# Plain output products set between the second block's first products of h, transposes ahead of the last rounding, and a pinned order with a pause on GpSimd

## The chip, the core and the metric

The kernel runs on one core of a Trainium2 chip. The core has TensorE (matrix products, PE in the profile; its weight loads are PEld), VectorE (DVE), ScalarE (ACT), GpSimd (POOL) and SyncE (SP), which here only issues DMAs. The metric is the device time of one execution in microseconds; lower is better.

## The reference

The input `x` is (8, 4096, 192), all float32. A causal convolution of 7 taps runs along the sequence, channel by channel, with one softmaxed set of taps for each of 8 heads; then a block of two matrices with silu between them:

```python
w = np.exp(weight - weight.max(-1, keepdims=True)); w = w / (w.sum(-1, keepdims=True) + 1e-9)
out = np.einsum('hk,bskhg->bshg', w, x_unf)      # 7 taps, zeros ahead of each sequence
h = out.reshape(32768, 192) @ w_in               # 192 -> 2048
g = h * (1.0 / (1.0 + np.exp(-h)))
return g @ w_out                                 # 2048 -> 192
```

The kernel takes the bits of the weights as they come, 64 bits to a word pair, and rounds them to float32 on the chip (`rounded`).

## The kernel before, in words

**Blocks.** The 32768 rows are 32 blocks of 1024 rows, each as two halves of 512 columns. For each block the rows are loaded (`ld`), transposed by VectorE so that channels lie on partitions (`i`, three of them), given the last 6 columns of the block before (`ha`, the halo: a copy and a small DMA), and convolved: tap 0 is ScalarE's, taps 1 to 6 are VectorE's (`v.ki` is tap i of channel part k; 18 on VectorE). The result is spread over both halves of the partitions by DMA (`sp.k`) and added up into five window sums (`w.0` to `w.5`).

**Products of h.** The first matrix is not multiplied plainly. Its 2048 columns are five groups (g = 0 to 4) and one plain piece; in each group 15 products (`Pr.g`) of combined weights with window sums or rows replace 18. A product has 64 rows of weights, so it occupies one half of TensorE's rows; the set `ON_B` (r = 0, 1, 2, 4, 5, 6, 11, 14, without 14 of group 4) says which products use the second half. The plain piece is `L`. The groups follow one another in the order of `QUEUE` (0, 4, 1, 2, 3). The products of a group build up in chains in PSUM, and between them ScalarE copies (`u`), VectorE adds (`X`, `a`, `b`, at L653) and ScalarE takes the silu (`S`, `SL`), which gives the tiles `g`. A bank of a group is written again two groups later, so a late addition holds up later products.

**Products of the output.** The second matrix is also combined: VectorE forms four differences for each quarter j of the columns (`t.ji`, L692), TensorE does six slots for each j and half e (`Di.je`, L724), and VectorE and ScalarE merge seven banks (`M`, `z`, `y`, `x`), transpose (`o`) and store (`st`).

**Block 0** goes another way, for the combined weights aren't ready: its convolution of the first two parts is done on TensorE (L977), its h by plain products (`up_plain`, L565, 192 records of TensorE), its output by plain products (`down_plain`, L743, 192 records). Meanwhile VectorE rounds the weights (`rounded`: four quarters of the input weights, then `round_out(0)` to `round_out(3)` for those of the output weights) and GpSimd combines them: 19 operations of 64x128 for each of five groups and 3 more for group 4 (`combine`), and 16 of 128x192 for the output weights (`combine_out`, which overwrite a part of `wo` that `down_plain` reads). All of GpSimd's combinations are at L353 (`comb`).

**The order** is written by hand. Each engine works through its own queue in the order in which the instructions were issued; instructions in `pin` keep the order of the program. `PLAN` is the steady order of one block's period; `START` is the order of the first blocks up to where `PLAN` begins. A token stands for block b = 2 in `START`; `-` ahead of it is block 1, `=` block 0 and `+` block 3, and the tokens that prepare input (`i`, `ha`, `v`, `sp`, `w`) act on the block after that. So `=v.21` is a tap of block 1, and `-P5.0` a product of block 1. `step` carries a token out. Before the change, `first_down` does all of block 0's plain output products at one place, when `START` comes to its first product; GpSimd's combinations are issued by `nc.gpsimd` without a pin, so that their place in GpSimd's queue is left to the scheduler.

Of the kernel before, what the change touches and what calls it, by code (L numbers as in the profile page):

```python
# [9 lines left out]
F32 = mybir.dt.float32  # L10
# [7 lines left out]
def kernel(  # L18
# [24 lines left out]
    nc = tc.nc  # L43
# [61 lines left out]
        "P7.3 | P11.3 b1.3 S3.3 sp.0 +v.10 | P8.2 a5.3"  # L105
    )
    START = (
        "=i.2 =i.0 =i.1 =ha.0 -ld.2 =v.00 =v.10 =v.01 -ld.1 =v.20 =v.11 =v.21 =v.12 -ld.0 "
        "=v.22 =v.23 =v.13 =v.14 =v.15 =v.02 =v.16 =v.24 =sp.1 =v.03 =v.25 =v.26 =v.04 =sp.2 "
        "=v.05 =v.06 -i.2 =sp.0 -i.0 ld.1 =w.0 =w.1 =o.0 -i.1 -L.01 -P5.0 =w.2 -ha.0 -L.02 "  # L110
        "-P5.4 -u5.0 =w.3 -P3.0 -P2.0 -u5.4 =w.5 =o.1 -L.00 -P2.4 -u4.0 =w.4 =st.1 -P6.0 "
        "-u4.4 -SL.0 -P6.4 -u2.0 -X2.0 -L.11 -u2.4 -L.10 -v.10 -P12.0 -P1.0 -v.11 -L.12 -u0.0 "
        "=o.2 -P9.0 -P1.4 -v.20 =st.2 -SL.2 -P13.0 -P0.0 -u0.4 -X4.0 -v.12 -P0.4 -P3.4 -u1.0 "
        "ld.0 -S2.0 -b1.0 -P7.0 -P14.0 -u1.4 -X2.4 -P11.0 -P10.0 -S3.0 -a5.0 =st.0 -P5.1 "
        "-P9.4 -S4.0 -b5.0 -v.13 -P12.4 -P4.0 -u5.1 ld.2 -X4.4 -v.00 -P2.1 -P14.4 -b1.4 -a1.0 "
        "-P7.4 -P11.4 -u4.1 -v.14 -S3.4 -P6.1 -P10.4 -S1.0 -v.21 -P8.0 -P5.2 -v.01 -u2.1 "
        "-S4.4 -a5.4 -P1.1 -P13.4 -u5.2 -a0.0 -SL.1 -P4.4 -b5.4 -u0.1 -P3.1 -S2.4 -P0.1 -a1.4 "
        "-P12.1 -X2.1 -P2.2 -u1.1 -v.22 -P9.1 -P14.1 -P8.4 -X4.1 -S3.1 -b1.1 -u4.2 -P7.1 "
        "-P5.3 -v.02 -S0.0 -P10.1 -P6.2 -a5.1 -a0.4 -P13.1 -P4.1 -u2.2 -v.23 -P3.2 -u5.3 "
        "-P1.2 -a1.1 -S2.1 -S0.4 -X2.2 -P2.3 -P8.1 -u0.2 -b5.1 -P11.1 -P9.2 -u4.3 -a0.1 -S1.1 "  # L120
        "-v.03 -P6.3 -P13.2 -S4.1 -P3.3 -P0.2 -X4.2 -u2.3 -v.04 -S2.2 -P12.2 -u1.2 -X2.3 "
        "-S5.0 -P7.2 -P11.2 -v.24 -S0.1 -P9.3 -P14.2 -b1.2 -S5.4 -a5.2 -S1.4 -P10.2 -P1.3 "
        "-S3.2 -v.25 -S5.1 -D0.00 -v.15 -S4.2 -v.05 -u0.3 -D1.00 -b5.2 -P0.3 -P13.3 -X4.3 "
        "-v.16 -P12.3 -P4.2 -u1.3 -t.00 -P11.3 -P7.3 -a1.2 -D1.20 -b1.3 -S1.2 -D0.11 -a5.3 "
        "-S2.3 -S4.3 -t.02 -D0.01 -S5.2 -D1.01 -v.26 -t.01 -D0.31 -v.06 -P10.3 -P14.3 -t.03 "
        "-P8.2 -P4.3 -S3.3 -sp.2 -D1.21 -a0.2 -a1.3 -D1.30 -b5.3 -sp.1 -D0.21 -t.10 -S5.3 "
        "-S0.2 -D4.00 i.1 -D3.01 i.0 +ld.2 i.2 -D4.01 -t.11 -D2.00 ha.0 -D2.01 -D0.20 -sp.0 "
        "-t.12 -D3.00 -t.13 v.00 -D5.00 v.20 P5.0 -P8.3 -D5.01 -a0.3 -D2.10 -t.20 -S0.3 +ld.0 "
        "-D5.11 -D4.10 -S1.3 v.21 v.10 -D1.10 u5.0 -w.0 -D2.11 -t.21 -D0.10 -w.1 -D3.10 v.01 "
        "v.11 -D4.11 -D5.10 -t.23 -D3.11 -D1.11 -t.22 -D4.21 v.12 -D2.21 -t.30 -D4.20 v.22 "  # L130
        "-D5.20 -D0.30 -t.31 -D2.20 -y0.0 v.02 P3.0 P2.0 -t.33 -D2.31 v.03 -D2.30 v.04 -D5.30 "
        "-w.2 -D1.31 -t.32 -D3.20 -w.3 -D5.31 -D5.21 v.23 -D4.30 -x2.0 u4.0 v.24 -D3.30 -x2.1 "
        "-z1.0 -w.4 -D3.31 -y2.0 -M1.0 -y1.0 -D3.21 v.05 -x2.2 -x0.0 -M3.0 P6.0 L.01 -M2.0 "
        "-D4.31 u2.0 -x2.3 X2.0 P12.0 P1.0 -M6.0 -w.5 P5.4 L.00 u0.0 -M4.0 L.02 P0.0 u5.4 "
        "v.25 P2.4 u1.0 b1.0 P14.0 u4.4 -M5.0 -x1.0 P6.4 P9.0 S3.0 v.13 P13.0 P5.1 u2.4 X4.0 "
        "SL.0 -o.1 P10.0 P1.4 S2.0 v.14 u5.1 L.11 b5.0 u0.4 L.12 v.06 L.10 P7.0 P0.4 v.15 "
        "SL.2 P12.4 P2.1 u1.4 a5.0 -M7.0 P11.0 P3.4 u4.1 P6.1 P14.4 S4.0 X2.4 S5.0 b1.4 P4.0 "
        "P13.4 u2.1 -o.2 S3.4 P1.1 P9.4 a1.0 v.16 P5.2 P8.0 u0.1 X4.4 P10.4 P0.1 u5.2 a0.0 "
        "P7.4 P2.2 b5.4 u1.1 S2.4 P3.1 P14.1 a5.4 u4.2 P12.1 P4.4 X2.1 S3.1 v.26 P11.4 P9.1 "
        "a1.4 P6.2 P13.1 -o.3 S4.4 X4.1 P5.3 P8.4 u2.2 b1.1 P11.1 P7.1 u5.3 sp.1 a0.4 SL.1 "  # L140
        "S2.1 P2.3 a5.1 P3.2 -o.0 P4.1 u4.3 P10.1 X2.2 -st.2 S4.1 P6.3 S1.0 a1.1 P9.2 b5.1 "
        "P1.2 u2.3 +ld.1 P8.1 X4.2 u0.2 +i.0 P12.2 S0.0 a0.1 P0.2 P13.2 t.00 -st.0 u1.2 P3.3 "
        "P1.3 S2.2 b1.2 P7.2 P11.2 -st.1 u0.3 X2.3 S1.4 P10.2 P14.2 +i.2 S4.2 a5.2 P0.3 P9.3 "
        "+i.1 P13.3 P4.2 u1.3 X4.3 +ha.0 S5.1 b5.2 P14.3 P7.3 a1.2 P11.3 P12.3 S3.3 sp.0 a5.3 "
        "S0.4 P8.2 b1.3 +v.10 -st.3"
    )
    QUEUE = (0, 4, 1, 2, 3)

    def pin(ins):
        return tc.keep_in_program_order(ins)  # L150
# [199 lines left out]
        )  # L350

    def comb(out, u, v, op):
        nc.gpsimd.tensor_tensor(out, u, v, op=op)  # L353

    PLAIN = (1, NJ - 1, 1)

# [243 lines left out]
    def chain_bank(g, c):  # L600
        return banks[(c * 2 + QUEUE.index(g) % 2) if c < 2 else 4]

    def product(b, g, r):
        e = int(r in ON_B and (g, r) != SWAP)
        if r in RIGHT:
            rhs = rows(wins[b], e)[:, RIGHT[r], :]
        else:
            rhs = rows(dups[b], e)[:, SLOT[e][X_OF[r]], :]
        if r in (13, 11):
            to, first = banks[XBANK[2 if r == 13 else 4]], False  # L610
        else:
            c = next(c for c in range(3) if r in CHAINS[c])
            to, first = chain_bank(g, c), r == CHAINS[c][0]
        pin(
            nc.tensor.matmul(  # L615
                to, raw(g, *LEFT[e][r], e), rhs, start=first, stop=True, skip_group_check=True
            )
        )

# [24 lines left out]
        free.append(us.pop(key))  # L644
        return free[-1]

    def sums_h(b, name, g):

        o = int(name[1:])
        t1, t2, t3 = (chain_bank(g, c) for c in range(3))  # L650

        def add(out_, u, v, op=ALU.add):
            pin(nc.vector.tensor_tensor(out_, u, v, op=op))  # L653

        if name[0] == "u":
            us[b, g, o] = free.pop(0)
            pin(nc.scalar.copy(us[b, g, o], t1))  # L657
        elif name[0] == "X":
            add(banks[XBANK[o]], used(b, g, o), t2)
        elif name[0] == "a":  # L660
            add(h_of(b, g, o), used(b, g, o), t2)
        elif name[0] == "b":
            c = us.get((b, g, o), None)
            c = h_of(b, g, o) if c is None else c
            add(c, c, t3, ALU.subtract)
        else:
            h = h_of(b, g, o)
            src = {3: t1, 2: banks[XBANK[2]], 4: banks[XBANK[4]]}.get(o, h)
            pin(nc.scalar.activation(h, src, AF.Silu))  # L669
# [24 lines left out]
    def out_slot(b, j, i, e, half=None):  # L694
# [24 lines left out]
        for q in range(4):  # L719
# [11 lines left out]
                )  # L731
            )

    def down_plain(b):

        acc = [bank() for _ in range(NK)]
        for j in range(NJ):
            for a in range(2):
                for e in range(2):
                    for k in range(NK):  # L740
                        for n in range(2):
                            pin(
                                nc.tensor.matmul(  # L743
                                    acc[k][R * n : R * n + R, :],
                                    wo[j][:, a, e, R * k : R * k + R],
                                    gs[b, j, a][:, n, e, :],
                                    start=j == 0 and a == 0 and e == 0,
                                    stop=j == NJ - 1 and a == 1 and e == 1,
                                )
                            )  # L750
                        yield
                del gs[b, j, a]
        cmb = xpool.tile([P, 4, TB], F32, tag="cmb", name="cmb")
        cmbs[b] = [cmb]
        for k in range(NK):
            pin(nc.scalar.copy(cmb[:, k, :], acc[k]))

    def merge(b, name, q):

# [74 lines left out]
    def step(b, token):  # L834
# [11 lines left out]
        did.add((b, token))  # L846
        digits = [int(c) for c in arg]
        if name[0] == "P":
            product(b, digits[0], int(name[1:]))
        elif name == "L":  # L850
            plain(b, *digits)
        elif name == "SL":
            silu_plain(b, *digits)
        elif name[0] in "uXabS":
            sums_h(b, name, digits[0])
        elif name == "t":
            sum_g(b, *digits)
        elif name[0] == "D":
# [6 lines left out]
            turn_out(b, *digits)  # L865
        elif name == "st":
            store_out(b, *digits)
        elif name == "ld":
            if b + 1 < NB:
                load(b + 1, digits)  # L870
# [144 lines left out]
    for j in range(NJ):  # L1015
# [7 lines left out]
        if j == 1:  # L1023
            load(1)
    for j in range(2, NJ):
        round_out(j)
    for g in (0, 1, 4, 2, 3):
        for e in range(2):
            combine(g, e)
    ahead = {"i", "ha", "v", "sp", "w"}  # L1030
    outs = {f"{t}.{k}" for t in ("o", "st") for k in range(NK)}
    did.update((0, t) for t in base if t.split(".")[0] not in ahead and t not in outs)

    def first_down():
        for _ in down_plain(0):
            pass
        for j in range(NJ):
            combine_out(j)
        banks.extend(bank() for _ in range(8))
        free.extend(upool.tile([P, TB], F32, tag="u", name="u") for _ in range(10))  # L1040

    begun = set()
    for t in START.split():
        if not banks and (t[:2] in ("-P", "-L", "=o")):
            first_down()
        step(2, t)
    for b in range(3, NB + 2):
        for s in plan:
# [34 lines left out]
```

## Time and profile before

| | |
|---|---|
| time, median of 3 runs | 2377.75 us (2377.5 to 2378.28) |
| the profiled execution | 2378.31 us, its span 2376.6 us |
| TensorE busy | 2366.9 us, granted clock 1.00 |
| VectorE busy | 2107.6 us |
| ScalarE, GpSimd busy | 1199.2 and 99.1 us |
| block 0's plain products of h | 19.1 to 60.5 us |
| block 0's plain output products | 60.4 to 101.8 us |
| block 1's products of h | 101.75 to 138.96 us |
| block 2's products of h | 183.76 to 220.53 us |
| GpSimd combining | 28.1 to 123.4 us |

Times in the profile count from the start of the span. A row of a timeline gives the start, the length, the engine, the line, the operation, output<-inputs, the shape, how many were merged into the row, and in brackets the idle time of the engine before it with what ended it. A matmul in float32 leaves two records. Rows of matmuls overlap where two run on unlike halves of the rows, and their ends are modelled, so a busy TensorE can still be half empty.

### The profile page before, as it was taken

The numbers are of one execution on the slowest core, as the hardware profiler recorded it, in microseconds if no ns is written. First come the engines' busy times: TensorE is split into PE (matmuls) and PEld (weight loads), VectorE is DVE, ScalarE is ACT, GpSimd is POOL, SyncE is SP. The second block draws the span as 40 slices with busy tenths as digits, with TensorE's granted clock in tenths as the row PEclk, the third lists the DMA queues.
The fourth block names the chain that finished last, engine by engine and source line by source line (L and its number), as shares of the span: only waits on it lengthen the run. The fifth ranks groups of instructions, "written<-read, shape, count | busy, mean of one in ns | idle before, by whom it ended". The sixth has DMA issues, their size and how long they took to land.

```text
span 2376.6 us, 44012 instructions
## 1 busy us (share of the span) xinstructions
PE 2366.9 (100%) x17630; PEld 1058.5 (45%) x17630; DVE 2107.6 (89%) x2877; ACT 1199.2 (50%) x2275; POOL 99.1 (4%) x167
## 2 busy tenths in 40 slices
PE   9999999999999999999999999999999999999998
PEld 4334444444444444444444444444444444444443
DVE  8898988998989989888998889888898988898866
ACT  5346544456444565444564445654446544456443
POOL 6900000000000000000000000000000000000000
PEclk9999999999999999999999999999999999999999
DMA  6422212222121222112221212221122212222111
GB/s 149 81 39 43 48 31 37 42 52 52 29 45 32 52 52 44 35 33 46 52 52 28 42 36 52 52 41 35 32 49 52 52 27 38 41 52 52 22 27 18
DMA packets 451245, 106.56 MB, mean 45 GB/s; under 512 B 423584, under 2 KB 428704, under 8 KB 451040
## 3 DMA queue, kind: packets, MB, share of 16 engines
q1 hardware_dynamic: 447392, 101.78, 23.3%
q8 instruction: 138, 2.26, 0.4%
q0 software_dynamic: 448, 1.58, 0.3%
q10 hardware_dynamic: 3200, 0.39, 0.1%
q14 instruction: 67, 0.55, 0.1%
HBM read 31.46 MB, written 25.17 MB: 24 GB/s over the span
## 4 chain that ended last, share of the span: by engine, by line
PE 99%; DVE 0%; ACT 0%; issue 0%; ACTq 0%
PE ps L724 47%; PE ps L615 43%; PE ps L627 4%; PE ps L743 2%; PE ps L565 2%; PE ps L977 1%; PE ps L417 0%; DVE nat L493 0%; DVE g L653 0%; DVE cmb L157 0%; ACT u L157 0%; DVE t L692 0%; DVE osb L157 0%; DVE ps L653 0%; DVE u L653 0%
## 5 line engine op out<-in xcount | busy, mean ns | idle before, releaser
L615 PE MATMUL ps<-win,ws 64*128 64x512 f32 x1550 | 699.3, 609 | 0.8 <-DVE ps L653 0.8
L724 PE MATMUL ps<-g,wo 128*32 128x512 f32 x2976 | 681.2, 592 | 0.0
L615 PE MATMUL ps<-win,wr 64*128 64x512 f32 x1550 | 636.8, 598 | 1.1 <-DVE g L653 1.1
L657 ACT COPY u<-ps 128x512 f32<-128x512 f32 x775 | 444.7, 586 | 284.3 <-PE ps L615 281.7
L724 PE MATMUL ps<-t,wo 128*32 128x512 f32 (+2 forms) x4528 | 524.2, 447 | 0.0
L724 PE MATMUL ps<-t,wx 128*32 128x512 f32 x2976 | 489.9, 592 | 0.6 <-DVE g L653 0.6
L493 DVE SCALAR_TENSOR_TENSOR nat<-xt,taps,nat 128x512 f32<-128x512 f32 x564 | 414.5, 754 | 5.8 <-ACT nat L490 4.3
L615 PE MATMUL ps<-dup,wr 64*128 64x512 f32 x868 | 412.6, 597 | 0.0
L669 ACT ACTIVATE g<-g 128x512 f32<-128x512 f32 x465 | 276.3, 628 | 182.7 <-DVE g L653 182.7
L692 DVE TENSOR_TENSOR t<-g,t 128x1024 f32<-128x1024 f32 x248 | 302.7, 1221 | 61.6 <-PE ps L724 60.5
L615 PE MATMUL ps<-dup,ws 64*128 64x512 f32 x682 | 338.5, 603 | 0.0
L692 DVE TENSOR_TENSOR t<-g 128x1024 f32<-128x1024 f32 x248 | 300.2, 1220 | 35.0 <-PE ps L724 31.7
L653 DVE TENSOR_TENSOR g<-u,ps 128x512 f32<-128x512 f32 x465 | 314.8, 682 | 15.2 <-PE ps L615 7.4
L615 PEld LDWEIGHTS ps<-win,wr 64*128 64x128 f32 x1550 | 239.0, 186 | 173.2 <-issue 96.3
L669 ACT ACTIVATE g<-ps 128x512 f32<-128x512 f32 x465 | 267.9, 598 | 90.4 <-PE ps L615 90.4
L780 ACT COPY yx<-ps 32x512 f32<-32x512 f32 x150 | 86.9, 579 | 423.9 <-PE ps L724 422.4
L615 PEld LDWEIGHTS ps<-win,ws 64*128 64x128 f32 x1550 | 245.4, 186 | 121.9 <-ACT u L657 62.2
L724 PEld LDWEIGHTS ps<-t,wo 128*32 128x32 f32 x4528 | 178.3, 110 | 244.3 <-issue 233.2
L653 DVE TENSOR_TENSOR ps<-u,ps 128x512 f32<-128x512 f32 x310 | 212.5, 686 | 40.5 <-PE ps L615 28.3
L724 PE MATMUL ps<-g,wx 128*32 128x512 f32 x1488 | 246.2, 594 | 0.0
L724 PEld LDWEIGHTS ps<-t,wx 128*32 128x32 f32 x2976 | 121.0, 110 | 261.2 <-issue 231.4
L724 PEld LDWEIGHTS ps<-g,wo 128*32 128x32 f32 x2976 | 169.3, 110 | 112.1 <-issue 112.1
(89 smaller groups left out, 1751.9 us busy)
## 6 DMA issues: line engine op xcount, KB each, us to landing
dup<-nat SPq DMA_DIRECT2D x345, 128.0 KB, 2.3
nat<-in_x_dram SPq DMA_DIRECT2D x382, 64.0 KB, 2.4
out_dram<-osb SPq DMA_DIRECT2D x376, 64.0 KB, 2.0
raw<-in_moe_w_out_dram SPq DMA_DIRECT2D x8, 384.0 KB, 3.5
raw<-in_moe_w_in_dram SPq DMA_DIRECT2D x12, 192.0 KB, 4.7
ws<-wr POOLq DMA_DIRECT2D x8, 192.0 KB, 3.0
raw<-in_moe_w_in_dram SPq DMA_DIRECT2D x6, 128.0 KB, 3.1
xt<-xt SPq DMA_DIRECT2D x31, 4.5 KB, 1.9
```

Source lines behind the costliest of these rows:

```text
L493: nc.vector.scalar_tensor_tensor(out=dst, in0=src, scalar=tap, in1=dst, op0=ALU.mult, op1=ALU.add)
L565: nc.tensor.matmul(hs[a, n, e], rows(wr[j], e)[:, a, k, :], rows(d, e)[:, n, k, :], start=k == 0, stop=k == NK - 1,)
L615: nc.tensor.matmul(to, raw(g, *LEFT[e][r], e), rhs, start=first, stop=True, skip_group_check=True)
L627: nc.tensor.matmul(banks[PLAIN_BANKS[n and 1 + e]][:, cols], rows(wr[j] if own == e else ws[j], e)[:, a, k, :], rows(dups[b], e)[:, SLOT[e ...
L653: pin(nc.vector.tensor_tensor(out_, u, v, op=op))
L657: pin(nc.scalar.copy(us[b, g, o], t1))
L669: pin(nc.scalar.activation(h, src, AF.Silu))
L692: pin(nc.vector.tensor_tensor(t[i // 2][:, i % 2, :], u, v, op=ALU.subtract))
L724: nc.tensor.matmul(accs[b][at][SQ * q : SQ * q + SQ, to], lhs[:, e, SQ * k : SQ * k + SQ], rhs[:, e, ts(q, TB // 4) if i == 5 else to], st ...
L743: nc.tensor.matmul(acc[k][R * n : R * n + R, :], wo[j][:, a, e, R * k : R * k + R], gs[b, j, a][:, n, e, :], start=j == 0 and a == 0 and e ...
L780: pin(nc.scalar.copy(to, acc[3 * (name[0] == "x") + k][n:P, :]))
L977: nc.tensor.matmul(by_pe[k][n], rows(diag, n)[:, k, i, :], rows(xts[0], n)[:, k, i : i + TB], start=i == 0, stop=i == K - 1,)
```

## The change

It has four parts.

1. Block 0's plain output products become tokens. `down_plain(0)` is a generator of 48 steps; `dp` takes one (the number in the token only keeps tokens apart). They write fixed banks (4, 5, 6 of the eight that the later products use) instead of three of their own, and the copies out of them are tokens (`cp.0` to `cp.2`) on ScalarE. 47 steps stand ahead of block 1's first products (`-L.01 -P5.0`), one after them. With the last step, `combine_out` is issued for all four quarters.
2. Block 1's transposes and halo (`i.0`, `i.1`, `i.2`, `ha.0`) are issued ahead of `round_out(3)` instead of after it.
3. GpSimd's combinations are pinned (`pool.tensor_tensor`). Groups 0, 4 and 1 are combined first; then the token `go.1` issues a copy on GpSimd that reads one column of block 1's convolved part k = 1 after its tap 6, so that GpSimd waits for that tap, and behind it groups 2 and 3; then the output weights.
4. The list `START` is written anew. It holds the same tokens of the later blocks in another order; nine taps and the transposes of block 2 now stand ahead of block 1's fourth pair of products. `PLAN` is not changed. Products and copies get an optional half width, which no token uses.

```diff
     START = (
-        "=i.2 =i.0 =i.1 =ha.0 -ld.2 =v.00 =v.10 =v.01 -ld.1 =v.20 =v.11 =v.21 =v.12 -ld.0 "
-        "=v.22 =v.23 =v.13 =v.14 =v.15 =v.02 =v.16 =v.24 =sp.1 =v.03 =v.25 =v.26 =v.04 =sp.2 "
-        "=v.05 =v.06 -i.2 =sp.0 -i.0 ld.1 =w.0 =w.1 =o.0 -i.1 -L.01 -P5.0 =w.2 -ha.0 -L.02 "
...
+        "=dp.31 =v.00 =v.10 =dp.45 =v.20 =dp.42 =dp.8 =dp.24 =dp.28 =dp.44 =dp.38 =dp.27 "
...
+        "=dp.17 -ld.0 =dp.2 =dp.19 -ld.1 =dp.34 =v.21 =dp.41 =v.11 =dp.21 =v.22 =dp.16 =v.01 "
+        "=v.23 =dp.40 =v.12 =dp.30 =v.24 =dp.23 =v.02 =v.25 =dp.20 =v.03 =dp.1 =v.26 =dp.13 "
+        "=v.04 =sp.2 =dp.10 =v.13 =v.05 =dp.6 =v.14 =dp.22 =v.06 =dp.29 =v.15 =sp.0 =dp.4 "
+        "=v.16 =go.1 =dp.12 -i.1 =sp.1 -i.2 =dp.47 -i.0 =dp.0 =dp.3 -ha.0 =dp.32 =dp.43 =w.0 "
+        "=dp.36 -v.20 -v.00 =w.1 =dp.14 -v.10 -v.21 =dp.5 -v.01 -v.11 -L.01 -P5.0 =w.2 =dp.9 "
+        "-u5.0 -v.12 -v.22 =cp.1 -P2.0 -L.00 =w.3 -P5.4 -L.02 -u4.0 -v.02 -P6.0 -P3.0 -SL.0 "
+        "=cp.0 -L.10 -u2.0 -L.11 -u5.4 -X2.0 -L.12 =cp.2 -P1.0 -v.13 =w.5 -P2.4 -P12.0 -u0.0 "
...
     def comb(out, u, v, op):
-        nc.gpsimd.tensor_tensor(out, u, v, op=op)
+        pool.tensor_tensor(out, u, v, op=op)
...
+    DOWN_BANKS = (4, 5, 6)
+
     def down_plain(b):
-        acc = [bank() for _ in range(NK)]
+        cmbs[b] = [xpool.tile([P, 4, TB], F32, tag="cmb", name="cmb")]
...
-                                    acc[k][R * n : R * n + R, :],
+                                    banks[DOWN_BANKS[k]][R * n : R * n + R, :],
...
+                        if (a, e, k) == (1, 1, NK - 1):
+                            for c in range(2):
+                                del gs[b, j, c]
+                            if j == NJ - 1:
+                                for c in range(NJ):
+                                    combine_out(c)
                         yield
...
+    def copy_plain(b, k):
+        pin(nc.scalar.copy(cmbs[b][0][:, k, :], banks[DOWN_BANKS[k]]))
...
+        elif name == "dp":
+            next(downs)
+        elif name == "cp":
+            copy_plain(b, *digits)
+        elif name == "go":
+            pool.tensor_copy(warm, nats[1][:, digits[0], 0, 0:1])
+            for g in (2, 3):
+                for e in range(2):
+                    combine(g, e)
...
     for j in range(2, NJ):
+        if j == NJ - 1:
+            for t in [*(f"i.{k}" for k in range(NK)), "ha.0"]:
+                step(0, t)
         round_out(j)
-    for g in (0, 1, 4, 2, 3):
+    for g in (0, 4, 1):
         for e in range(2):
             combine(g, e)
...
-    def first_down():
-        for _ in down_plain(0):
-            pass
-        for j in range(NJ):
-            combine_out(j)
-        banks.extend(bank() for _ in range(8))
-        free.extend(upool.tile([P, TB], F32, tag="u", name="u") for _ in range(10))
-
-    begun = set()
+    banks.extend(bank() for _ in range(8))
+    free.extend(upool.tile([P, TB], F32, tag="u", name="u") for _ in range(10))
+    downs, begun = down_plain(0), set()
     for t in START.split():
-        if not banks and (t[:2] in ("-P", "-L", "=o")):
-            first_down()
         step(2, t)
```

## The prediction

> **What bounds the kernel now.** I read the page first: how busy each engine is and the chain that ended last. TensorE is busy for 2366.9 of 2376.6 us, so a change that leaves the matmul work alone can win only what TensorE loses while it looks busy, and the few microseconds in which it is idle.
>
> ```profile
> span 2376.6 us, 44012 instructions
> PE 2366.9 (100%) x17630; PEld 1058.5 (45%) x17630; DVE 2107.6 (89%) x2877; ACT 1199.2 (50%) x2275; POOL 99.1 (4%) x167
> ...
> PE 99%; DVE 0%; ACT 0%; issue 0%; ACTq 0%
> ```
>
> Then the waits of TensorE over the whole span. Only two idle times lie in the stretch that the change rewrites (1.1 and 0.8 us, at 123.6 and 118.7); the 1.1 on `warm` is the start and the 0.6 lies at the end.
>
> ```profile
> PE ps L417 <- DVE warm L157: 1.1, 1, 1.1
> PE ps L615 <- DVE g L653: 1.1, 1, 1.1
> PE ps L615 <- DVE ps L653: 0.8, 1, 0.8
> PE ps L724 <- DVE g L653: 0.6, 1, 0.6
> ```
>
> Then the timelines of VectorE and TensorE around there (start, length, operation, idle time before and what ended it). VectorE is what TensorE waited for, and these rows say why it was late.
>
> ```profile
> 78.23 1.89 DVE L459 STREAM_TRANSPOSE xt<-nat 128x512 f32<-128x512 f32 x3
> 82.96 16.27 DVE L493 SCALAR_TENSOR_TENSOR nat<-xt,taps,nat 128x512 f32<-128x512 f32 x18 [2.85 <-ACT nat L490]
> ...
> 101.56 0.95 DVE L527 TENSOR_TENSOR win<-dup 128x512 f32<-128x512 f32 x1 [1.11 <-DMA dup<-nat]
> ...
> 115.81 2.25 DVE L493 SCALAR_TENSOR_TENSOR nat<-xt,taps,nat 128x512 f32<-128x512 f32 x1
> ...
> 138.27 2.07 DVE L493 SCALAR_TENSOR_TENSOR nat<-xt,taps,nat 128x512 f32<-128x512 f32 x3
> ```
>
> The 18 taps of block 1 take 0.90 us each while GpSimd combines weights; three taps at 138.27, with GpSimd done, take 0.69 each. One tap at 115.81 takes 2.25: three of GpSimd's 128x192 operations lie in it (0.58, 0.59 and 0.59 us, from 115.82 on).
>
> ```profile
> 60.40 41.42 PE L743 MATMUL ps<-g,wo 128*64 128x512 f32 x192
> ...
> 118.72 0.69 PE L615 MATMUL ps<-win,ws 64*128 64x512 f32 x1 [0.78 <-DVE ps L653]
> ...
> 123.60 1.29 PE L615 MATMUL ps<-win,wr 64*128 64x512 f32 x3 [1.09 <-DVE g L653]
> ```
>
> Last, how much TensorE loses while busy. A product of h uses one half of the rows and leaves two records of 0.43 us; two products on unlike halves run together, so one costs 0.43 us in a pair. TensorE's timeline gives three unbroken stretches of products:
> - block 1, 101.75 to 138.96: 37.2 us for 70 product-equivalents, 29.9 at 0.4275 each. Lost 7.3, of which 1.9 idle.
> - block 2, 183.76 to 220.53: 36.8 for 73, that is 31.2. Lost 5.6.
> - block 3, under the steady plan, 257.95 to 293.33: 35.4 for 79, that is 33.8. Lost 1.6.
>
> So the two hand-ordered stretches lose 5.7 and 4.0 us more than the steady one. That is nearly all there is to win, about 9.7 us of 2377.
>
> **The change, part by part.**
>
> *Transposes and halo ahead of the last rounding.* Today: the transposes end at 80.12, the halo's DMA is issued at 80.19 and lands 1.9 us later, ScalarE's first tap starts at 82.20 and VectorE's at 82.96, after 2.85 us idle. Afterwards the transposes run from about 71.5, the last rounding ends 1.89 later, at 80.1, and the halo (one DMA, and one for the tail, 0.62 us of SyncE each) and the three first taps on ScalarE (0.65 each) lie under it. VectorE's taps start at 80.1: **2.85 us won on VectorE**. On ScalarE the head's 0.19 us copy goes ahead of the rounding's two operations; its tail landed long before. On SyncE twelve loads for block 2 (6.44 us of issuing) follow, done by about 82, before the first duplicate wants the queue. If block 1's rows weren't in by 71, the rounding would wait behind the transposes; today they are asked for between 38.4 and 45.4 and take some 3, so nothing is booked.
>
> *GpSimd's order and its pause.* Combinations become pinned: groups 0, 4, 1 (60 operations), then `go`, which waits for tap 6 of k = 1, the last of the 18, then groups 2 and 3 (38), then the 16 of the output weights, which wait for the last plain output product. Queued behind `go` are those 54; products of groups 2 and 3 and the D steps wait for them. Today 53 operations end between 28.09 and 79.46, 0.97 us each with their DMAs; 60 end near 86.3. So 7 of the 18 taps still pay 0.90 and 11 pay 0.69: taps from 80.1 to 94.0, against 99.2 today. The pause is worth 11 x 0.21 = **2.3 us on VectorE** (1.3 if the pitch is the 0.78 of the six dependent taps at 12.94).
>
> Those 54 operations then fall on the products of block 1. From 100.0 to 115.8 GpSimd does 25 operations at 0.63 us, from 115.8 to 123.4 ten at 0.76. From 94.2 on: 8 before 99 at 0.58, 11 at 0.85 while taps and window sums lie thick (the 0.87 of 86 to 99), 19 at 0.65, 16 at 0.76 give group 2 at 108, group 3 at 120.5, output weights at 133. They are wanted at about 117 (P5.2), 124 (P5.3), each by the products ahead of it at 0.43 from 101, and 138 (D1.20, D1.31: `wx` of j = 2, 3; 75 product-equivalents from 101.8 on, 32.1, and some 4 of loss). Bounds for the end: 126 (0.55 and 0.67) and 141 (0.87 and 1.0). **No wait** booked; up to 3 us.
>
> *What the moved work costs VectorE: rule against row.* The Trainium skill, "SBUF — State Buffer", section "Who interferes with whom", says a VectorE instruction with two SBUF inputs and a GpSimd one that reads SBUF exclude each other, the second blocking fully. By that a contended tap costs 0.69 + 0.53 (GpSimd's undisturbed pitch at 100) = 1.22. The row says 0.90, so overlap is partial; the 2.25 us tap is the rule to the letter. Additions with one operand in PSUM don't suffer: 0.60 apart at 113 to 115 beside GpSimd, and 0.60 after it. So I cost block 1's stretch in VectorE time. Before: 32.1 us of undisturbed steps from the first window sum (101.56) to the first D, in 37.4 us, so 3.3 of contention, 2.6 of that in the four taps beside the ten output operations, and 2.0 idle. After: 17 taps instead of 13, four more additions and one transpose less, 36.7 us. Contention: at the average of before (3.3 in 22 us) 33 us of it give 5.2; counted by kind (11 taps x 0.2, six sums x 0.15, 16/10 of 2.6) it is 7.2; by the rule 23 x 0.53 = 12.2. The first window sum starts at 97.3 (94.0, two duplicate issues of 0.77, and the 1.7 that today's has). Ends: 97.3 + 36.7 + 2 idle + 5.2 = 141.2, or 143.2, or by the rule 148.2. Today's kernel at the same point of its work (4.6 us further than 138.96) would be at 143.5. **VectorE is 2.3 or 0.3 us ahead at the end of the stretch; by the rule 4.7 behind.** I take 2.0, near the first: the last taps aren't wanted by the D steps, so part of any lag dies there.
>
> *Order of the products.* Cut each stretch from its front into pairs of unlike halves (products 0, 1, 2, 4, 5, 6, 11, 14 use the upper half, the plain ones and the rest the lower). Before, 3 products of block 1 and 4 of block 2 stay alone; after, 2 and 1. One alone costs 0.43. The one in block 1 is swallowed while VectorE sets the pace; the three in block 2 give **1.3 us**. Other waits inside block 2's stretch I leave as they are: its VectorE work is 30.8 us against 30.5.
>
> *Plain output products between.* 47 of 48 steps of 0.86 stay ahead of block 1's first pair, one follows it. No work is removed; two more changes of tile shape at 0.1 us each (0.53 instead of 0.43 between starts, as at 101.76): **0.2 us lost**. Their three banks are now those that the last silus of block 0 free; the third step comes 1.7 us after 60.5, its silu ends by 61.6: nothing to 1.1 us. The three copies (0.59 each) stand among ScalarE's copies instead of ahead of them; banks 4 to 6 are wanted 5 us later. Half-width products and the pinned `comb` change no other instruction: no list uses a half.
>
> **Sum**: 2.0 + 1.3 - 0.2 = 3.1 us. Profiled execution: 2378.31 (span 2376.6 and 1.7 around it) becomes 2375.2. The median, 2377.75, lies 0.6 below that execution, so the forecast for it is **2374.7**. A measurement can tell about 0.2%, 4.8 us.
>
> **Rivals.**
> - *TensorE sets the pace again* (27%). Block 1's stretch loses only what the steady one does: idle 1.9 and 2.5 hidden, pairs 1.7, minus 0.2: 5.9, that is 2371.9. For it: taps end 5 us earlier. Against it: today's stretch is VectorE's (32.1 of 37.2 us undisturbed), and the new one has 36.7 in about 38.
> - *The stall only moves* (13%). The output operations, all sixteen now beside block 1's last taps, take back what the pause gave: 0.3 - 0.2, 2377.6. For it: both idle times of today lie beside ten of them. Against: the D steps behind need less of VectorE (38.8 us of work instead of 43.1).
> - *GpSimd is late* (5%), on the other side. The D steps wait for `wx` of j = 2 and 3. It decides once its 54 operations after `go` average over (138 - 94.2) / 54 = 0.81 us, and each 0.1 beyond costs 5.4. At 0.97, the pitch beside the rounding, they end at 146.6: 8.6 lost, 3.1 won, 2383.3. Against: 0.63 and 0.76 in that very stretch.
>
> **How the numbers follow.** The forecast, a gain below 4.8 us, has 55%, and its own range is 2373 to 2377. With the moved stall, 68% lie within 0.2%; faster by more 27%; slower by more 5%. The range goes from 2370.8 (all of the first rival and one microsecond more of hidden waits) to 2378.8 (the moved stall and a bank wait of 1.1).
>
> **What would show it.** VectorE's taps of block 1 start near 80 with no idle time ahead and end near 94; GpSimd is idle from about 86 to 94 and ends near 133; the last plain output step comes after two products of h. TensorE's idle times at 118 and 123 shrink or move to 120 to 135; block 2's stretch is about 1.3 us shorter. I am wrong if TensorE waits for `wx` or `ws` from GpSimd, if an idle time stands at 61, or if block 2's stretch doesn't shorten: then the pairs don't matter and other waits set it.

## The result, and the profile after

| | before | after |
|---|---|---|
| median of 10 runs | 2377.78 us (2377.50 to 2378.28) | 2371.45 us (2371.23 to 2371.95) |
| ratio, 95% interval | | 0.9973 (0.9964 to 0.9983) |
| profiled execution, its span | 2378.31, 2376.6 us | 2371.36, 2369.3 us |
| TensorE busy | 2366.9 us | 2361.4 us |
| GpSimd combines from, to | 28.1, 123.4 us | 43.3, 128.8 us |
| taps of block 1 on VectorE | 82.96 to 99.23 us | 75.32 to 90.95 us |

The kernel is 6.3 us faster, 0.27%. The forecast was 2374.7, its range 2370.8 to 2378.8. The time is inside the range, but it lies at the first rival's (2371.9), not in the case held likeliest (2373 to 2377).

The waits of TensorE over the whole span, after. Both idle times at 118 and 123 are gone.

```profile
PE ps L421 <- DVE warm L161: 1.1, 1, 1.1
PE ps L739 <- DVE g L666: 0.6, 1, 0.6
```

The timeline of VectorE, after. The transposes stand ahead of the last rounding, the taps follow it without idle time, and they still cost 15.63 / 18 = 0.87 us each, next to 0.90 before. They start 7.6 us earlier, though, where 2.85 had been booked.

```profile
66.07 1.88 DVE L463 STREAM_TRANSPOSE xt<-nat 128x512 f32<-128x512 f32 x3
...
75.32 15.63 DVE L497 SCALAR_TENSOR_TENSOR nat<-xt,taps,nat 128x512 f32<-128x512 f32 x18
90.99 1.90 DVE L463 STREAM_TRANSPOSE xt<-nat 128x512 f32<-128x512 f32 x3
94.12 0.81 DVE L531 TENSOR_TENSOR win<-dup 128x512 f32<-128x512 f32 x1 [1.23 <-DMA dup<-nat]
...
106.06 0.69 DVE L666 TENSOR_TENSOR ps<-u,ps 128x512 f32<-128x512 f32 x1 [2.52 <-ACT u L672]
```

The last row shows VectorE waiting 2.5 us for a copy of ScalarE in block 1's stretch: there it is no longer VectorE that sets the pace. The timeline of GpSimd tells where the earlier start comes from. Before, it combined from 28.1 on and issued its fourth pair of weight transfers only at 70.7:

```profile
28.09 1.52 POOL L353 TENSOR_TENSOR ws<-ws 64x128 f32<-64x128 f32 x2 [3.63 <-DMA ws<-wr]
...
70.68 1.05 POOL L341 DMA_DIRECT2D ws<-wr  x2
```

After:

```profile
41.88 1.38 POOL L345 DMA_DIRECT2D ws<-wr  x2 [5.33 <-DVE wr L161]
43.33 3.22 POOL L161 TENSOR_TENSOR wr<-wr 64x128 f32<-64x128 f32 x4
...
93.27 0.45 POOL L161 TENSOR_TENSOR ws<-ws,wr 64x128 f32<-64x128 f32 x1
93.78 0.18 POOL L161 COPY warm<-nat 128x1 f32<-128x1 f32 x1
93.92 2.59 POOL L161 TENSOR_TENSOR wr<-wr 64x128 f32<-64x128 f32 x4
```

The pinned combinations start at 43.3, behind the fourth pair of weight transfers, and GpSimd is busy with groups 0, 4 and 1 until 93.7. The copy that was to make it wait for the last tap finds that tap done 2.8 us ago and waits for nothing: **there is no pause**. What there is instead is a quiet stretch from 28 to 43, in which VectorE rounds two quarters of the input weights. One such quarter takes 6.6 us in quiet (28.31 to 34.91) and took 8.9 beside GpSimd before (28.48 to 37.41). The rows are the first of one quarter and of the next, before and after:

```profile
28.48 1.54 DVE L157 TENSOR_SCALAR two<-raw 128x768 int32<-128x768 int32 x2
...
37.41 1.55 DVE L157 TENSOR_SCALAR two<-raw 128x768 int32<-128x768 int32 x2
```

```profile
28.31 1.02 DVE L161 TENSOR_SCALAR two<-raw 128x768 int32<-128x768 int32 x2
...
34.91 1.02 DVE L161 TENSOR_SCALAR two<-raw 128x768 int32<-128x768 int32 x2
```

TensorE's stretches in its timeline, after: block 1's products from 100.34 to 137.91, the D steps (with eight products among them) to 178.57, block 2's products to 213.84. The first rows of these stretches and of what follows them, before:

```profile
101.75 0.69 PE L627 MATMUL ps<-dup,ws 64*128 64x512 f32 x1
...
138.96 1.06 PE L724 MATMUL ps<-g,wo 128*32 128x512 f32 x8
...
183.76 0.69 PE L615 MATMUL ps<-win,wr 64*128 64x512 f32 x1
...
220.53 0.63 PE L724 MATMUL ps<-g,wx 128*32 128x512 f32 x3
```

After (the row at 101.40 is the last plain output step):

```profile
100.34 0.69 PE L640 MATMUL ps<-dup,ws 64*128 64x512 f32 x1
...
101.40 1.08 PE L760 MATMUL ps<-g,wo 128*64 128x512 f32 x4
...
137.91 0.63 PE L739 MATMUL ps<-g,wx 128*32 128x512 f32 x3
...
178.57 0.69 PE L640 MATMUL ps<-dup,ws 64*128 64x512 f32 x1
...
213.84 0.63 PE L739 MATMUL ps<-g,wx 128*32 128x512 f32 x3
```

Counted at the prediction's prices (0.4275 us for each product-equivalent, 0.86 for a D step, some 0.25 for a narrow one). For block 2 the count is put right: its stretch holds 76 product-equivalents before and 77 after. The prediction has 73; it left out the three products with which `PLAN` opens, which run ahead of block 2's first D step.

| what TensorE loses in | before | after |
|---|---|---|
| block 1's products | 37.2 - 29.9 = 7.3 | 37.6 - 32.9 - 1.1 = 3.6 |
| the D steps of block 1 | 44.8 - 43.2 = 1.6 | 40.7 - 39.8 = 0.9 |
| block 2's products | 36.8 - 32.5 = 4.3 | 35.3 - 32.9 = 2.4 |

The 1.1 is the last plain output step with its two changes of tile shape. The losses fall by 6.3 us, less 0.2 for those changes: 6.1 of the 6.3 by which the medians differ. The two spans differ by 7.3. Of the rest, 0.6 lies ahead of all this, in how long the warm-up matmuls ran in these two executions (last section), and 0.6 behind block 2's stretch, from whose end to the end of the span it is 2156.1 us before, 2155.5 after and 2155.3 to 2156.0 in the other runs. Stretches are therefore counted from the first product of block 1, and times are the medians.

### The profile page after: what moved, and what is told of

Its sections match the earlier page's. It is cut to its first block, busy times and chain, and to the rows that moved or that the text cites. A ratio compares the mean times of both kernels' runs of the same rounds, so it can differ in the third digit from the quotient of the medians.

```text
span 2369.3 us, 44036 instructions
## 1 busy us (share of the span) xinstructions
PE 2361.4 (100%) x17630; PEld 1061.7 (45%) x17630; DVE 2101.8 (89%) x2877; ACT 1199.8 (51%) x2275; POOL 95.4 (4%) x168
## 4 chain that ended last, share of the span: by engine, by line
PE 99%; DVE 0%; ACT 0%; issue 0%; ACTq 0%; DVEq 0%
PE ps L739 48%; PE ps L623 43%; PE ps L640 4%; PE ps L760 2%; PE ps L569 2%; PE ps L1008 1%; PE ps L421 0%; DVE cmb L161 0%; ACT u L161 0%; DVE g L666 0%; DVE t L707 0%; DVE osb L161 0%; DVE xt L463 0%; PE ps L447 0%; ACTq L942 0%
## 5 line engine op out<-in xcount | busy, mean ns | idle before, releaser
L739 PE MATMUL ps<-t,wo 128*32 128x128 f32 (+2 forms) x4528 | 523.8, 447 | 0.0
L666 DVE TENSOR_TENSOR g<-u,ps 128x512 f32<-128x512 f32 x465 | 315.1, 682 | 15.2 <-PE ps L623 7.3
```

What stands on the lines that cost most here:

```text
L739: nc.tensor.matmul(accs[b][at][SQ * q : SQ * q + SQ, to], lhs[:, e, SQ * k : SQ * k + SQ], rhs[:, e, ts(q, TB // 4) if i == 5 else to], st ...
```

## The experiments

The theory formed on the two traces: the pause does nothing; pinning moves GpSimd away from the first roundings; the lists do the rest. Its rivals are the forecast's mechanism (the pause), the new list alone, and a late GpSimd. The kernel before, run again beside each group of these runs, had medians of 2377.83 to 2377.97 us.

**Without the wait.** In the changed kernel:

```diff
         elif name == "go":
-            pool.tensor_copy(warm, nats[1][:, digits[0], 0, 0:1])
             for g in (2, 3):
```

> The changed kernel without the copy that makes GpSimd wait for block 1's last tap; groups 2 and 3 are issued at the same place. Theory A (the pause never happens: the changed kernel's GpSimd is still busy with group 1 until 93.8 and the copy at 93.78 waits for nothing, so what helps is that GpSimd starts at 43.3 instead of 28.1): no change, 2371.4 us within 0.5, taps of block 1 still about 15.6 us for 18. Theory B (the pause shortens the taps by 2.3 us of VectorE, as forecast): 1 to 2 us slower, 2373.

Measured: 2371.13 us (2370.85 to 2371.87), 0.3 below the changed kernel with ranges that overlap, so not distinguishable from it; 18 taps in 15.64 us. The copy is worth nothing, as theory A has it.

**The pin alone.** In the kernel before:

```diff
     def comb(out, u, v, op):
-        nc.gpsimd.tensor_tensor(out, u, v, op=op)
+        pool.tensor_tensor(out, u, v, op=op)
```

> The kernel before with one edit: GpSimd's combinations are pinned, so all of them stand behind the fourth pair of weight transfers in its queue. The queues of the other engines are the same as before. Theory A (late start of GpSimd): combining starts near 43 instead of 28, the last rounding ends near 73.5 instead of 78.2, the taps of block 1 end near 94.5, both idle times of TensorE at 118 and 123 go and block 1's stretch of products shortens by about 3 us: 2374.8 us. Theory B (the new list is what helps): within 1 us of before, 2377. Theory C (GpSimd now late): output weights end near 130, TensorE waits for wx or ws, slower than before.

Measured: 2375.26 us (2374.94 to 2375.90), 2.6 us faster than before (ratio 0.9988, 0.9981 to 0.9995). The timeline of VectorE in this run:

```profile
74.34 1.89 DVE L459 STREAM_TRANSPOSE xt<-nat 128x512 f32<-128x512 f32 x3
79.07 15.63 DVE L493 SCALAR_TENSOR_TENSOR nat<-xt,taps,nat 128x512 f32<-128x512 f32 x18 [2.85 <-ACT nat L490]
...
97.03 0.83 DVE L527 TENSOR_TENSOR win<-dup 128x512 f32<-128x512 f32 x1 [1.11 <-DMA dup<-nat]
```

TensorE comes to block 1's first D step at:

```profile
136.69 1.06 PE L724 MATMUL ps<-g,wo 128*32 128x512 f32 x8
```

The transposes come 3.9 us earlier than before and the first window sum 4.5, with nothing changed but GpSimd's queue. Block 1's stretch shortens from 37.2 to 34.7 (102.00 to 136.69); the later ones stay at 44.8 and 36.8. Of the 1.9 us of idle time in it 0.6 is left. Theory C is out: the output weights end at 126.3, and TensorE waits for none of them.

**Pin and early transposes, old list.** As above, and:

```diff
     for j in range(2, NJ):
+        if j == NJ - 1:
+            for t in [*(f"i.{k}" for k in range(NK)), "ha.0"]:
+                step(0, t)
         round_out(j)
```

> The kernel before with two edits: combinations pinned, and block 1's transposes and halo ahead of the last rounding; the list of the order is the old one. Theory A (once GpSimd starts late, VectorE is far enough ahead and a further 2.85 us of lead is worth nothing to TensorE): equal to the pin alone within 0.7 us. Theory B (each microsecond of VectorE's lead counts in block 1's stretch): 2 us faster than the pin alone.

Measured: 2374.85 us (2374.64 to 2375.65). The first window sum moves from 97.03 to 93.20:

```profile
93.20 0.97 DVE L527 TENSOR_TENSOR win<-dup 128x512 f32<-128x512 f32 x1 [1.12 <-DMA dup<-nat]
```

The time falls by 0.4 us, of which block 1's stretch in the trace shows only 0.1 (34.7 to 34.6): with the old list the lead that the pin gave was enough.

**The same edit undone with the new list.** The four lines are taken back in the changed kernel: the loop is `for j in range(2, NJ): round_out(j)`, and the `for t in [...]` follows it.

> The changed kernel with block 1's transposes and halo put back behind the last rounding. VectorE idles 2.85 us again and the taps of block 1 end near 93.9 instead of 91.0. Theory A (VectorE's lead is larger than TensorE needs, as with the old list, where the same edit moved the block by 0.1 us): within 0.7 us of the changed kernel, 2371.4. Theory B (the new list, which puts nine taps of block 2 ahead of the first products, needs that lead): 1.5 to 3 us slower, 2373 to 2374.5.

Measured: 2373.11 us (2372.59 to 2373.48), 1.7 us slower than the changed kernel: the lower edge of B. VectorE waits longer for ScalarE's first taps than the 2.85 us of the kernel before, and its first window sum comes 4.3 us later than in the changed kernel:

```profile
79.89 15.04 DVE L497 SCALAR_TENSOR_TENSOR nat<-xt,taps,nat 128x512 f32<-128x512 f32 x18 [4.14 <-ACT nat L494]
...
98.39 0.69 DVE L531 TENSOR_TENSOR win<-dup 128x512 f32<-128x512 f32 x1 [1.52 <-DMA dup<-nat]
```

Block 1's stretch grows from 37.6 to 38.7 (100.40 to 139.08). The new list puts nine taps of block 2 ahead of block 1's fourth pair, three of them first taps on ScalarE and six on VectorE, and with it the lead that the early transposes give counts. The same edit is worth 0.4 or 1.7 us by the order around it.

**The new order from the D steps on, alone.** In the kernel before, only the list differs:

```diff
     START = (
         "... -P1.3 -S3.2 -v.25 -S5.1 "
-        "-D0.00 -v.15 -S4.2 -v.05 -u0.3 -D1.00 ..."
+        "-v.15 -v.05 -u0.3 -P0.3 -b5.2 -S4.2 -P4.2 -P12.3 ... -P7.3 ... -D1.01 -S3.3 -t.00 -D1.20 ..."
```

> The kernel before with one edit: from block 1's first D step on, the list follows the order of the new one; up to there it is the old one, and nothing is pinned. Theory A (the pairs of unlike halves): block 2's stretch of products, 36.8 us before, shortens by 1.3 to 1.9 us and nothing changes before 139 us: 2376. Theory B (block 2 is shorter in the changed kernel because VectorE comes to it earlier): 2377.7, no change.

Measured: 2376.42 us (2376.16 to 2377.01), 1.5 us faster than before, with a ratio that reaches 1 (0.9984 to 1.0002). Block 2's stretch in TensorE's timeline:

```profile
184.21 0.69 PE L627 MATMUL ps<-dup,ws 64*128 64x512 f32 x1
...
219.47 0.63 PE L724 MATMUL ps<-g,wx 128*32 128x512 f32 x3
```

35.3 us, what the changed kernel has, though VectorE is as late as before and GpSimd starts at 28.6. So block 2's gain of 1.9 us is the order alone, as theory A has it; that the pairs are what counts in the order is not shown by this run. The run as a whole gains less, for seven products that stood among the D steps now stand in block 1's stretch, and it shows four idle times of TensorE there, 3.1 us in all (1.2 for a weight from GpSimd).

**All but block 1's own list and the split.** The kernel before with pin, early transposes and that same tail. GpSimd keeps the old order of its groups (0, 1, 4), without `go`.

> The kernel before with the pin, the transposes ahead of the last rounding and the new order from block 1's first D step on; block 1's own products keep the old list and the plain output products stay in one piece. Theory A (the gains of the parts add up: 3.0 of pin and transposes, 1.5 to 2.7 of the tail): 2372.2 to 2373.3, so that 0.8 to 1.9 us are left for block 1's new list and the split. Theory B (the tail needs the new head): no better than pin and transposes alone, 2374.8.

Measured: 2374.16 us (2373.93 to 2374.86), only 0.7 better than pin and early transposes. The gains do not add up. D steps (40.7) and block 2 (35.3) have what they have in the changed kernel, but block 1's stretch, with the same 77 product-equivalents as there, takes 39.5 us (101.05 to 140.53), a loss of 6.6 instead of 3.6:

```profile
140.53 0.63 PE L724 MATMUL ps<-g,wx 128*32 128x512 f32 x3
```

So 2.7 us of the result come from the new list of block 1 with the split and the order of groups that goes with it. Added in this order, pin, early transposes, tail and head give 2.6, 0.4, 0.7 and 2.7 us. The new list of block 1 with the old tail was not run.

**Unpinned again.** The changed kernel with `nc.gpsimd.tensor_tensor` in `comb`.

> The changed kernel with GpSimd's combinations unpinned again, all else kept. Theory A (the late start is worth 2.5 us, as the pin alone showed): combining starts near 28, the last rounding ends near 80 instead of 75.3, 2374 us. Theory B (the new list alone makes block 1's stretch fast): within 0.7 us of the changed kernel, 2371.4.

Measured: 2377.46 us, and the runs scatter: two of twelve near 2374, as A says, five between 2376.0 and 2377.6, five between 2379.4 and 2380.1. Slower, but by more than the rounding explains. TensorE in the profiled execution (2379.87, one of the slowest):

```profile
108.20 1.22 PE L623 MATMUL ps<-dup,wr 64*128 64x512 f32 x1 [4.78 <-POOL wr L357]
121.80 0.69 PE L623 MATMUL ps<-win,ws 64*128 64x512 f32 x1 [1.05 <-DVE ps L666]
```

Left to the scheduler, GpSimd combines output weights from 82.0 and 96.2 on, while the group that the new list wants at 103 isn't done: 4.8 us idle. So the pin also keeps the order in which TensorE asks for weights. What differs in the faster runs of this version was not profiled.

**A real pause.** In the changed kernel:

```diff
-    for g in (0, 4, 1):
+    for g in (0, 4):
...
         elif name == "go":
             pool.tensor_copy(warm, nats[1][:, digits[0], 0, 0:1])
-            for g in (2, 3):
+            for g in (1, 2, 3):
```

> The changed kernel with group 1 moved behind the wait for block 1's last tap, so that the pause is real: GpSimd has 41 operations ahead of it, ends them near 79 and waits to the taps' end. Thirteen taps then cost 0.69 instead of 0.87, taps end near 88.6 instead of 91.0. Theory A (more lead of VectorE is worth nothing, and GpSimd's 73 operations behind the pause end near 137, so that group 3 and the output weights come just in time or late): 2371.4 to 2373.5. Theory B (the pause, once real, is worth what was forecast for it): 1 to 2 us faster, 2370.

Measured: 2372.02 us (2371.17 to 2372.35), 0.6 slower than the changed kernel. VectorE's timeline and GpSimd's:

```profile
75.36 13.15 DVE L497 SCALAR_TENSOR_TENSOR nat<-xt,taps,nat 128x512 f32<-128x512 f32 x18
```

```profile
88.72 0.18 POOL L161 COPY warm<-nat 128x1 f32<-128x1 f32 x1 [9.51 <-DVE nat L497]
```

Now GpSimd waits 9.5 us and the taps are 2.5 us shorter, the size that the forecast gave the pause. TensorE doesn't get it: block 1's stretch is 38.3 us, not 37.6. Theory A, in that the lead is worth nothing; what makes the stretch 0.7 longer is not shown, for weight loads that wait for GpSimd come to 1.0 us here and to 1.3 in the changed kernel.

**The plain output products in one piece.** The changed kernel with `=dp.9` moved ahead of `-L.01 -P5.0`.

> The changed kernel with the last plain output step ahead of block 1's first pair, so that the plain output products are one piece again. Theory A (two changes of tile shape at 0.1 us are all that the split costs, and it hides nothing): 0.2 us faster, 2371.2. Theory B (the split covers a wait of block 1's first products on VectorE or ScalarE): slower by up to 0.9, 2372.3.

Measured: 2371.87 us (2371.38 to 2372.18), 0.4 slower, with ranges that overlap. TensorE idles where the step had been:

```profile
102.86 0.69 PE L623 MATMUL ps<-win,wr 64*128 64x512 f32 x1 [0.71 <-ACT u L672]
```

The next product, P2.0, waits for ScalarE's copy of P5.0, whose bank it writes. The split step fills that wait, which is theory B; its size of 0.4 us is hardly more than the 0.3 by which the run without the copy differs the other way.

**Could the rest be had?** Block 1's stretch still loses 3.6 and block 2's 2.4, where the steady plan loses 1.6 (the expectation for the first run has 3.6 for block 2, by the count put right above). Two runs let the plan set the order earlier, at `L.02` of block 2, and right after block 1's first pair (there the loop starts at 1, and the list ends with `=dp.9 -u5.0 =cp.0 =cp.1 =cp.2`):

```diff
-    for b in range(3, NB + 2):
+    for b in range(2, NB + 2):
         for s in plan:
```

> The changed kernel with its list cut where block 2's products of h begin; from there on the steady plan, unchanged, sets the order of block 2 too. Theory A (what block 2's stretch still loses, 3.6 us against 1.6 under the steady plan, is a matter of the order in the list): the stretch shortens by 1 to 2 us, 2369.5 to 2370.5. Theory B (block 2 comes to it with its inputs later than a steady block, so the plan's order waits more): 35.3 us or longer, 2371.4 to 2373.

> The changed kernel with its list cut after block 1's first pair of products and the last plain output step; the copies of the plain output follow, and the steady plan sets the order of all of blocks 1 and 2. Theory A (order alone): both stretches come near the steady loss of 1.6 us, 2368 to 2369.5. Theory B (block 1's window sums and GpSimd's weights come too late for the plan, in which they are ready a block ahead): block 1's stretch is longer than 37.6 us and TensorE shows idle time in it, 2372 to 2376.

Measured: 2372.80 (2372.48 to 2373.58) and 2374.70 us (2372.80 to 2375.98), both slower than the changed kernel. In the first, block 2's stretch is 36.7 us, with 0.8 idle at 183.2 on a sum of VectorE. In the second, block 2's is 35.4, the very length of the steady block 3, so the plan's order can do it when a block comes to it in the plan's own state; but block 1's products take until 144.7, and TensorE idles there:

```profile
105.00 0.66 PE L589 MATMUL ps<-win,ws 64*128 64x512 f32 x1 [0.71 <-issue]
111.34 0.69 PE L589 MATMUL ps<-win,ws 64*128 64x512 f32 x1 [1.65 <-DVE ps L632]
```

Theory B in both. Of the versions run none is clearly faster than the changed kernel.

**How late a start?** The pin alone, with groups 0, 1 and 4 issued right behind block 0's products:

```diff
         up_plain(0, j)
+        for g, k in ((0, 0), (1, 1), (4, 2)):
+            if j == k:
+                for e in range(2):
+                    combine(g, e)
...
-    for g in (0, 1, 4, 2, 3):
+    for g in (2, 3):
```

> The pin alone (the kernel before with pinned combinations), with groups 0, 1 and 4 issued right behind block 0's plain products that use their weights, so that in GpSimd's queue they stand behind the third pair of weight transfers instead of the fourth; combining should start near 36.5 instead of 43.3 (28.1 in the kernel before). The queues of VectorE, ScalarE and TensorE hold the same instructions in the same order. Theory A (what the pin wins is the rounding without GpSimd beside it): the last rounding ends in between, near 74.5 where the pin alone has 72.5 and the kernel before 76.4 (each 1.9 ahead of the end of the transposes), and the time lies in between, 2376 to 2377. Theory B (the start doesn't matter, the pin wins by the order in which groups are finished): as the pin alone, 2375.3 within 0.4.

Measured: 2375.32 us (2374.69 to 2375.80), equal to the pin alone. GpSimd starts at 36.5 and VectorE's lead lies in between (transposes from 76.9, first window sum at 99.4), as A said, but the time is B's. (The expectation's 72.5 and 76.4 for the end of the last rounding are each 1.8 us too early: it ends where the transposes start, at 74.3 and 78.2.)

```profile
99.39 0.85 DVE L527 TENSOR_TENSOR win<-dup 128x512 f32<-128x512 f32 x1 [1.11 <-DMA dup<-nat]
```

So 2.2 us of lead at the first window sum do as much for the old list as 4.5. The traces place what the pin wins. Counted from block 1's first product, the tap that took 2.25 us before starts after 14.1 us there and after 13.0 in both pinned runs; the three taps behind the next additions start after 18.0 and after 15.6. So 1.1 us are won ahead of that tap and 1.3 at it, for it takes 0.95 and 0.91 us in the pinned runs (none in block 1's stretch is above 1.08). Together that is nearly the 2.5 by which the stretch is shorter. In the kernel before, the first of TensorE's two idle times hangs on that tap: it ends at 118.06, the addition behind it at 118.66, and TensorE goes on at 118.72. Whether the 1.1, and the absence of the long tap, come from a first part of the lead or from the order of the groups stays open: the edit moved the start and the order together, and no run parts them.

## Why the prediction was right or wrong

*Transposes ahead of the last rounding.* Right: the 2.85 us of idle are gone. Their worth depends on what follows, 0.4 us with the old list and 1.7 with the new.

*The pause.* Wrong, and this is the step that failed: "60 end near 86.3". It carried over the start at 28.09 and the mixed order of the unpinned queue. GpSimd's queue also holds four pairs of weight transfers, and I did not ask where pinned work would stand against them. It stands behind the last, which waits for a rounding that ends at 41.6. So GpSimd was 15 us later and never paused. In place of 2.3 us from the taps, VectorE got about 4.8 from the rounding (82.96 - 75.32, less 2.85; 3.9 with the pin alone). With both in hand (the real pause) the taps' share brought nothing.

*Cost of the moved work.* The question was whether VectorE would be 2.3 or 0.3 us ahead in block 1's stretch. At the first window sum it was 7.4 us ahead of before (94.12 against 101.56), where 4.3 had been reckoned, and it waited for ScalarE. The rule of full exclusion, which would have made the change slower, doesn't hold as a price here: taps beside the sixteen output operations took 1.04, 1.06 and 1.10 us, less than 0.69 and the 0.59 of one such operation together. The 2.25 of before did not come again, so counting it as typical (2.6 us for ten operations) was too dark. (A slip in the sum, 3.3 in 22 us makes 5.0 in 33 us and not 5.2, changes nothing.) Block 1's stretch lost 3.6 instead of 7.3; 2.0 had been booked for 3.7.

*Pairs.* Right in sign and place, small in size: 1.3 booked, 1.9 measured, and shown to be the order alone by the run that changed the tail alone. The 0.6 beyond the count of lone products was not traced, and that lone products make the rest is argued, not shown.

*Split of the plain output.* Probably the wrong sign: 0.2 lost was booked for two changes of shape; they cost that, but the step fills a wait of 0.7, and the split gains 0.4 by the medians. I had looked for waits on VectorE there and not on the first copy of ScalarE.

*D steps.* Not booked: the new order breaks them three times for products instead of five, four changes of shape fewer at 0.1, which explains 0.4 of the 0.7 that the stretch lost less (0.9 instead of 1.6).

*GpSimd late.* The rival's premise was not met: 54 operations from 93.9 to 128.8 average 0.65 us, below the 0.81 from which it was to decide. TensorE does wait for GpSimd in the unpinned run, where the order is wrong and not the pace.

*Sum.* 3.1 forecast, 6.3 measured. That the time lies in the range is in good part luck: VectorE got its lead from the rounding and not from the pause, and what of it TensorE could use was set by the list. The case "TensorE sets the pace again" (27%) is nearest, with 5.9, but its terms miss and cancel: it gives block 1's stretch 4.8 (1.9, 2.5 and one lone product), block 2's 1.3 and the D steps nothing, where 3.7, 1.9 and 0.7 were measured. The table of lost time was the right frame with one wrong count. With 76 product-equivalents block 2's stretch lost 4.3 and not 5.6, so 8.4 us and not 9.7 lay above the steady plan; the two stretches won 5.6 of them.

## What to carry to other kernels

Pinned work stands behind what was issued to that queue before it, here from 28.1 to 43.3 us: find the last wait ahead of it before giving the work a start time. Compare stretches by what they lose against their own count of work; that shows whether an engine's lead is worth anything before one pays for it, and here about the same lead (3.8 and 4.3 us at the first window sum) was worth 0.4 us with one order and 1.7 with another. When two edits touch the same queue, run each alone and both together, for their gains need not add up.

## What the runs showed of the hardware that was not expected

Rounding and combining slow each other somewhat more than taps and combining do. A quarter's rounding took 6.6 us alone and 8.9 beside GpSimd, 35% more; a tap took 0.69 alone and 0.87 to 0.90 beside it, 26 to 30% more. GpSimd's 64x128 operations took 0.45 us in quiet, mostly 0.78 to 0.90 beside taps and up to 1.18 beside roundings. Additions of block 1's stretch, which have one operand in PSUM, keep a pitch of 0.60 beside GpSimd (from 124.30 to 126.09 after). GpSimd started 15.2 us later and ended only 5.4 later; that this is why is argued from these rows, no run shows it alone.

The four warm-up records after the taps' small product took 1.83 us before and 1.11 after, with a granted clock of 1.00 in both, and 1.11 to 2.05 in the other runs; all that follows on TensorE shifts by up to 0.9 us from one execution to another. A comparison of a few tenths by spans of single executions would have read this as an effect of the change.
